# Batch 1's second product by Strassen's algorithm, with the loads, transposes and read-outs around it put in another order

## The chip, the cores and the metric

One core of one Trainium2 chip runs the kernel. The time is device microseconds of one execution; the figure compared is the median over runs. Beside each set of runs one execution is profiled, and the views below are of that one.

The engines are named as in the profile: PE is TensorE (PEld its weight loads), DVE is VectorE, ACT is ScalarE, POOL is GpSimd, SP is SyncE. SP and POOL issue DMAs in their own instruction order.

## The reference

Cross attention between tokens and a small state, and then a feed-forward layer with exact Gelu, over all rows that the attention gives.

```python
B, H, S, Ns, D = 8, 8, 512, 32, 64
scores  = x @ state^T / 8            # per batch and head, S x Ns
xread   = softmax(scores)  @ state   # S x D
scores2 = state @ x^T / 8            # Ns x S
sread   = softmax(scores2) @ x       # Ns x D
rows    = concat([xread, sread], rows).reshape(8 * 544, 512)
out     = gelu(rows @ w_in) @ w_out  # w_in 512 x 2048, w_out 2048 x 512
```

## The kernel before, in words

All matrix operands are bf16, sums are fp32 in PSUM. The kernel never forms xread. For each batch b it forms P = state x w_in, head by head (256 rows for pairs of heads and states, 2048 columns, `Ps[b]`), and multiplies the softmax weights by it: hidden = A x P.

The steps of one batch are these.

- `load_x` (L115, a DMA that POOL issues and that casts to bf16), `rearr` (L214, POOL, into `x4`), `xtr_dma` (L269, a transpose by DMA that SP issues, into `xT`), and `rearr_ones` (L223, POOL for batch 2 and later, into `xo`, the operand of the read-out). There are two `xb` buffers, so batch b + 2 is loaded when `rearr` and `rearr_ones` of batch b are done.
- `load_st` and `state_prep` (L149): state, transposed by PE and put into `sbd` by DVE.
- `scores` (L316): x times state on PE; ACT takes exp into `e`. Exp and Gelu need different tables of ACT, so two table loads surround it.
- `norm` (L338): sum, reciprocal and product on DVE, giving the weights `a`; `atr` (L354, PE and DVE, batches 0 and 1) or `atr_dma` (L364, a transpose by DMA that SP issues) turns them into A^T.
- P in four chunks f of 512 columns: `p_mm` (L409) issues eight small matmuls in a 64x32 tiling of PE into two PSUM banks, `p_copy` (L424) copies one on ACT and one on DVE. Several chunks in a row are a P run (`burst`, L435, and `p_run`, L796).
- `M(m)` (`mm1`, L473): the first product, sixteen column blocks m of 128 per batch, each two matmuls of 512 columns on PE and one Gelu on ACT, into `gs[b]`.
- the second product, gs[b] x w_out. Batches 0 and 1 do it plainly: `U(u)` (`mm2`, L499) is four matmuls of 512 columns for a quarter q of the sum and a row block j; `mm2_m` (L527) does the same numbers by column block m. Units 0 to 15 are batch 0, 16 to 31 are batch 1. Each row block is copied by DVE (L491) and written out by SP. Batches 2 to 7 do it by Strassen's algorithm: `X(b, name)` (L611), seven products named 1 to 7, of sixteen matmuls of 256 columns each. `g_sum` (L577, DVE) makes the sums of quarters of gs[b] that five of them need, and `w_sums` (L554, DVE) the five sums of quarters of w_out, once.
- `sread` (L372): the read-out of the state rows, 32 small matmuls in a 128x32 tiling; `sread_out` (L386, DVE) divides by the sums, and `srt` (L399, PE and DVE) transposes into `XSR`, which is multiplied by w_in and w_out for all batches together in the course of batch 7.

PSUM has eight banks. Four rotate (`ftile`, tag f: M, scores, read-outs, transposes, some P chunks), so an instruction that takes a bank waits until the one four back has been read. Four have names (`otile`, o0 to o3: the second product and the other P chunks).

The order on every engine is written out by hand in the body: engines run their instructions in that order and wait where an operand or a buffer isn't ready. The start loads w_in and w_out in chunks on POOL's queue; from batch 2 on a loop over b and eight steps p does `M(k, k + 1)` in each step and hangs the rest on it: for the next batch, nb = b + 1, scores in p = 1, norm in p = 2 and 3, P runs in p = 5 and 7, and for the last batch its products X in p = 0 to 4. `hold` is a one-element POOL copy that reads a Gelu output, so that the loads behind it start no earlier.

Of the kernel before, what the change touches and what calls it, by code (L numbers as in the profile page):

```python
# [17 lines left out]
def kernel(  # L18
# [8 lines left out]
    nc = tc.nc  # L27

    B, H, S, D = x.shape
# [73 lines left out]
    def load_w_in(f0, f1):  # L103
        for t in range(2):
            nc.gpsimd.dma_start(  # L105
                out=w_in_bf[64 * t:64 * t + 64, :, f0:f1],
                in_=moe_w_in[256 * t:256 * t + 256, f0:f1].rearrange("(c d) f -> d c f", c=HC),
            )
# [3 lines left out]
    def load_w_out(i):  # L112
        nc.gpsimd.dma_start(out=w_out_bf[:, 4 * i:4 * i + 4, :], in_=w_out_r[:, 4 * i:4 * i + 4, :])
# [6 lines left out]
    def load_st(b0, b1):  # L120
        nc.gpsimd.dma_start(
            out=st_bf[:, b0:b1, :, :].rearrange("q b t d -> q (b t) d"),
            in_=st_rows[:, b0:b1, :, :].rearrange("q b t d -> q (b t) d"),
        )
# [7 lines left out]

    def load_rest():
        load_w_out(1)
        for f in range(2, FC):
            load_w_in(512 * f, 512 * f + 512)
            load_w_out(f)
        load_st(2, B)
        load_x(2)
        load_x(3)  # L140


# [289 lines left out]

    def burst(chunks, b_read=None):  # L435
        done = []
        first = len(chunks) < 4 and b_read is not None
        if first:
            sread(b_read)
        for i, (b, f) in enumerate(chunks):  # L440
            done.append((b, f, p_mm(b, f, ftile if i < 2 else otile)))
        for x in done[:2]:
            p_copy(*x)
        if b_read is not None and not first:
            sread(b_read)
        for x in done[2:3]:
            p_copy(*x)
        if b_read is not None:
            sread_out(b_read)
        for x in done[3:]:  # L450
            p_copy(*x)


    def pmat00(h):
        if h == 0:
            Ps[0] = att.tile([128, 2, d_ff], BF16, name="P", tag="P")
# [42 lines left out]
    def mm2(b, q, j):  # L499
        if q == 0:  # L500
            ops[b, j] = otile([128, d_model], "op")
        ps = ops[b, j]
        for m in range(4 * q, 4 * q + 4):
            nc.tensor.matmul(  # L504
                ps,
                lhsT=gs[b][:, m, j * 128:(j + 1) * 128],
                rhs=w_out_bf[:, m, :],
                start=(m == 0),
                stop=(m == MC - 1),
            )  # L510
        if q == 3:
            rows = out_rows(b, j)
            evac(ps, [(rows, slice(0, 128), 0, d_model)])

    def mm1_sr(m):
        hp = ps_f.tile([128, B * NS], FP32, name="hps", tag="f")
# [276 lines left out]
            nc.vector.tensor_tensor(out=rs["o", 0][:, :NH], in0=ps, in1=rs["u"], op=add)  # L793
            r_out(0)

    def p_run(b, fs, banks):  # L796
        done = []
        for f, at in zip(fs, banks):
            it = iter(at or ())
            tiles = (lambda shape, name: otile(shape, name, next(it))) if at else ftile  # L800
            done.append((b, f, p_mm(b, f, tiles)))
        for x in done:
            p_copy(*x)


    def M(*ms):
# [77 lines left out]
    srt(0)  # L884
    U(4, 5)
    rearr_ones(1)
    U(6)
    pmat(0, 2)
    norm(1, 0)
# [4 lines left out]
    sread_out(1)  # L894
    M(10, 11)
    mm2_m(0, 8)
    mm2_m(0, 9)
    burst([(0, 3), (1, 0)])
    mm2_m(0, 10)
    atr(1)  # L900
    M(12, 13)
    srt(1)
    M(14, 15)
    mm2_m(0, 11)
    begin(2)
    rearr(2)
    xtr_dma(2)
    rearr_ones(2)
    U(12)
    burst([(1, 1), (1, 2)])  # L910
    U(13)
    state_prep(2, B)
    M(16, 17)
    U(14)
    M(18, 19)
    U(15)
    burst([(1, 3), (2, 0), (2, 1)])
    U(16)


    M(20, 21)
    U(17)
    nc.gpsimd.tensor_copy(out=hold, in_=gs[1][:, 4, 0:1])
    load_x(4)
    w_sums(0)
    pmat(2, 2)
    begin(3)
    rearr(3)
    xtr_dma(3)
    rearr_ones(3)  # L930
    M(22, 23)
    scores(2, 0)
    scores(2, 1)
    U(18)
    norm(2, 0)
    norm(2, 1)
    M(24, 25)
    U(19)
    M(26, 27)
    U(20, 21)  # L940
    w_sums(1)
    M(28, 29)
    w_sums(2)
    U(22)
    atr_dma(2)
    M(30, 31)
    U(23)
    pmat(2, 3)
    w_sums(3)
    w_sums(4)  # L950

    u = 24
    for b in range(2, B):
        nb = b + 1
        for p in range(8):
            k = 16 * b + 2 * p
            if p == 1 and nb < B:
                scores(nb, 0)
                scores(nb, 1)
            if p in (2, 3) and nb < B:  # L960
                norm(nb, p - 2)
            if p == 3 and nb + 1 < B:
                xtr_dma(nb + 1)
            if p == 5 and nb < B:
                atr_dma(nb)
            if p == 6 and nb < B:
                srt(b)
            if p == 7 and nb == B - 1:
                srt(nb)
            M(k, k + 1)  # L970
            if b == 2:
                for _ in range(2 if p < 4 else 1):
                    if u < 32:
                        U(u)
                        u += 1
            elif p < 5:
                if p == 0:
                    g_sum(b - 1, "5")
                X(b - 1, "45127"[p])
                if p < 3:  # L980
                    g_sum(b - 1, "127"[p])
            if nb == B and p < 4:
                for m in range(4 * p, 4 * p + 4):
                    mm1_sr(m)
            if p == 1 and nb < B:
                sread(b)
                sread_out(b)
            if p == 4 and nb == B - 1:
                sread(nb)
                sread_out(nb)  # L990
            if p == 0 and b + 3 < B:
                nc.gpsimd.tensor_copy(out=hold, in_=gs[b][:, 0, 0:1])  # L992
                load_x(b + 3)
            if p == 0 and nb + 1 < B:
                begin(nb + 1)
                rearr(nb + 1)
            if p == 2 and nb + 1 < B:
                rearr_ones(nb + 1)
            if nb == B:
                if p == 4:  # L1000
                    r_homes()
                    r_sum("5")
                    r_sum("2")
                if p == 5:
                    g_sum(b, "6")
                    R("3")
                    r_sum("1")
                    R("4")
                    r_sum("6")
                    r_sum("7")  # L1010
                if p == 6:
                    R("5")
                    X(b, "3")
                    R("2")
                    R("1")
                if p == 7:
                    R("6")
                    X(b, "6")
                continue
            if p == 5:  # L1020
                g_sum(b, "6")
                if nb < B:
                    p_run(nb, (0, 1), ((0, 1), (3, 2)))
            if p == 6:
                X(b, "3")
            if p == 7:
                if nb < B:
                    p_run(nb, (2, 3), ((1, 2), None))
                X(b, "6")
    b = B - 1  # L1030
    for name in "521":
# [39 lines left out]
```

## Time and profile before

| | us |
|---|---|
| median of 8 runs | 206.97 |
| lowest and highest | 206.28, 207.75 |
| the profiled execution | 207.45 |
| its span, first to last instruction | 205.7 |
| PE busy | 198.6 |
| DVE busy | 138.2 |
| ACT busy | 132.8 |
| POOL busy | 62.2 |

The profiled execution has 1.75 us around its span. The granted PE clock is 1.0 throughout. PE's busy time is modelled from overlapping matmuls: the time that a matmul really takes from PE is read from the distance between the starts of neighbours. Every time in the views counts from the start of the span.

### The profile page before, as it was taken

The numbers are of one execution on the slowest core, as the hardware profiler recorded it, in microseconds if no ns is written. First come the engines' busy times: TensorE is split into PE (matmuls) and PEld (weight loads), VectorE is DVE, ScalarE is ACT, GpSimd is POOL, SyncE is SP. The second block draws the span as 40 slices with busy tenths as digits, with TensorE's granted clock in tenths as the row PEclk, the third lists the DMA queues.
The fourth block names the chain that finished last, engine by engine and source line by source line (L and its number), as shares of the span: only waits on it lengthen the run. The fifth ranks groups of instructions, "written<-read, shape, count | busy, mean of one in ns | idle before, by whom it ended". The sixth has DMA issues, their size and how long they took to land.

```text
span 205.7 us, 4708 instructions
## 1 busy us (share of the span) xinstructions
PE 198.6 (97%) x1971; PEld 130.8 (64%) x1979; DVE 138.2 (67%) x219; ACT 132.8 (65%) x240; POOL 62.2 (30%) x69
## 2 busy tenths in 40 slices
PE   8689999999999999999999999999999999999994
PEld 7444444444454567766775777667775788778893
DVE  2843675785739848995699858765878553165883
ACT  3874675679794879575956787587747566744120
POOL 8955300746063005720677006500220002200000
PEclk9999999999999999999999999999999999999999
DMA  6999999689664908745682502460106001030125
GB/s 198 185 174 203 206 198 194 108 235 132 128 76 124 248 13 102 158 149 59 71 173 92 129 0 78 100 183 3 53 3 204 3 0 51 3 153 0 54 94 162
DMA packets 40261, 23.14 MB, mean 113 GB/s; under 512 B 21808, under 2 KB 38320, under 8 KB 40240
## 3 DMA queue, kind: packets, MB, share of 16 engines
q0 software_dynamic: 13936, 8.10, 29.2%
q1 hardware_dynamic: 25616, 14.36, 27.7%
q10 hardware_dynamic: 688, 0.39, 0.6%
q8 instruction: 15, 0.25, 0.5%
q14 instruction: 6, 0.05, 0.1%
HBM read 17.30 MB, written 8.91 MB: 127 GB/s over the span
## 4 chain that ended last, share of the span: by engine, by line
PE 86%; DMA 7%; POOL 4%; issue 1%; DVE 0%; POOLq 0%
PE xp L586 34%; PE hp L478 25%; PE op L504 9%; DMA w_out_bf<-in_moe_w_out_dram 6%; PE p_ps L415 4%; PE hps L518 3%; PE rp L762 3%; POOL w_in_bf L105 2%; PE xp L692 2%; PE op L531 2%; DMA AT<-a 2%; PE pt L324 1%; PE sr L378 1%; POOL sbd L95 1%; POOL a L309 0%
## 5 line engine op out<-in xcount | busy, mean ns | idle before, releaser
L485 ACT ACTIVATE g<-hp 128x512 bf16<-128x512 f32 x124 | 67.2, 604 | 29.8 <-PE hp L478 24.6
L478 PE MATMUL hp<-AT,P 128*128 128x512 bf16 x248 | 63.6, 379 | 0.1
L586 PEld LDWEIGHTS <-gsum 128*128 128x128 bf16 x448 | 43.4, 98 | 11.3 <-issue 2.1
L580 DVE TENSOR_TENSOR gsum<-g 128x2048 bf16<-128x2048 bf16 x30 | 39.8, 1346 | 0.1
L478 PEld LDWEIGHTS <-P 128*128 128x128 bf16 x248 | 22.7, 98 | 18.9 <-ACT P L426 0.5
L586 PE MATMUL xp<-ws,gsum 128*128 128x256 bf16 x256 | 30.6, 273 | 0.0
L427 DVE CAST P<-p_ps 128x512 bf16<-128x512 f32 x31 | 20.0, 684 | 15.0 <-PE p_ps L415 15.0
L504 PE MATMUL op<-w_out_bf,g 128*128 128x512 bf16 x90 | 22.9, 379 | 0.4 <-DMA w_out_bf<-in_moe_w_out_dram 0.2
L586 PE MATMUL xp<-ws,g 128*128 128x256 bf16 x192 | 22.9, 273 | 0.0
L586 PE MATMUL xp<-w_out_bf,gsum 128*128 128x256 bf16 x192 | 22.8, 273 | 0.0
L426 ACT CAST P<-p_ps 128x512 bf16<-128x512 f32 x31 | 17.0, 604 | 7.9 <-PE p_ps L415 7.9
L586 PEld LDWEIGHTS <-g 128*128 128x128 bf16 x192 | 18.8, 98 | 4.3
L635 POOL TENSOR_TENSOR u<-s,oh 128x512 f32<-128x512 f32 x5 | 6.3, 1266 | 48.6 <-ACT oh L632 48.6
L504 PEld LDWEIGHTS <-g 128*128 128x128 bf16 x96 | 9.1, 98 | 11.5 <-issue 1.4
L218 POOL COPY x<-xb 128x1024 bf16<-128x1024 bf16 x12 | 12.6, 1082 | 10.9 <-DMA xb<-in_x_dram 10.9
L228 POOL COPY xo<-xb 128x1024 bf16<-128x1024 bf16 x12 | 14.5, 1242 | 1.3 <-PE sr L378 1.3
L347 DVE TENSOR_TENSOR a<-e,ics 128x512 bf16<-128x512 bf16 x14 | 13.8, 987 | 0.5
L344 DVE TENSOR_REDUCE cs<-e 128x16 f32<-128x512 bf16 x14 | 9.5, 675 | 2.8 <-ACT e L331 2.8
L629 DVE TENSOR_TENSOR s<-xp,s 128x512 f32<-128x512 f32 x5 | 3.5, 692 | 11.0 <-PE xp L586 11.0
L605 POOL TENSOR_TENSOR v<-q,oh 128x512 f32<-128x512 f32 x5 | 6.4, 1285 | 14.6 <-ACT oh L637 14.6
L415 PE MATMUL p_ps<-w_in_bf,sbd 64*32 64x512 bf16 x248 | 10.3, 382 | 0.0
L992 POOL COPY hold<-g 128x1 bf16<-128x1 bf16 x3 | 0.8, 278 | 29.7 <-ACT g L485 29.7
(111 smaller groups left out, 223.1 us busy)
## 6 DMA issues: line engine op xcount, KB each, us to landing
xb<-in_x_dram POOLq DMA_DIRECT2D x7, 512.0 KB, 7.6
out_dram<-oh SPq DMA_DIRECT2D x13, 256.0 KB, 2.4
out_dram<-osb SPq DMA_DIRECT2D x10, 256.0 KB, 3.2
out_dram<-oh SPq DMA_DIRECT2D x5, 512.0 KB, 2.7
w_out_bf<-in_moe_w_out_dram POOLq DMA_DIRECT2D x4, 512.0 KB, 12.5
w_in_bf<-in_moe_w_in_dram POOLq DMA_DIRECT2D x6, 256.0 KB, 12.4
x0f<-in_x_dram SPq DMA_DIRECT2D x3, 256.0 KB, 4.1
w_in_bf<-in_moe_w_in_dram POOLq DMA_DIRECT2D x4, 128.0 KB, 4.2
```

Source lines behind the costliest of these rows:

```text
L218: nc.gpsimd.tensor_copy(out=A.x4[:, :, :, 64 * t:64 * t + 64].rearrange("p j c d -> p c j d"), in_=src[:, t],)
L228: eng.tensor_copy(out=A.xo[:, :, :, 2 + 64 * t:66 + 64 * t].rearrange("p j c d -> p c j d"), in_=src[:, t],)
L344: nc.vector.reduce_sum(out=cs, in_=e4, axis=AX.X)
L347: nc.vector.tensor_tensor(out=A.a[:, :, hs].rearrange("p g (c n) -> p g c n", n=NS), in0=e4, in1=ics[:, :, :].to_broadcast((128, G, 2, NS) ...
L415: nc.tensor.matmul(ps[t][32 * c:32 * c + 32, :], lhsT=sbd[64 * t:64 * t + 64, b, c, 32 * t:32 * t + 32], rhs=w_in_bf[64 * t:64 * t + 64, c ...
L426: nc.scalar.copy(out=dst[:, 0, :], in_=ps[0])
L427: nc.vector.tensor_copy(out=dst[:, 1, :], in_=ps[1])
L478: nc.tensor.matmul(hp, lhsT=Ps[b][:, t, m * 128:(m + 1) * 128], rhs=atts[b].AT[:, :, t, :], start=(t == 0), stop=(t == 1),)
L485: nc.scalar.activation(out=gs[b][:, m, :], in_=hp, func=AF.Gelu)
L504: nc.tensor.matmul(ps, lhsT=gs[b][:, m, j * 128:(j + 1) * 128], rhs=w_out_bf[:, m, :], start=(m == 0), stop=(m == MC - 1),)
L580: nc.vector.tensor_tensor(out=t, in0=g_q(b, h0, k0), in1=g_q(b, h1, k1), op=op)
L586: nc.tensor.matmul(ps[:, j - js[0], :], lhsT=lhs[:, m, 128 * j:128 * j + 128], rhs=rhs[:, m, :], start=(first and j == js[0] and m == 0), ...
```

## The change

Batch 1's second product leaves the plain form (units 16 to 31) and takes the seven products X(1, ...), two of them ahead of the loop and five in the loop's first pass. The order of loads, P chunks, sums of w_out and transposes ahead of the loop is rewritten: state of batch 2 and x of batch 2 are loaded ahead of the last chunk of w_out, x of batch 3 behind it, the states of batches 3 to 7 later; the transpose of x of batch 3 stands ahead of that of A of batch 2. x of batches 4 and 5 is loaded in the loop's first pass, in p = 0 and p = 6. In the loop the read-out moves from p = 1 (and, for batch 7, p = 4) to p = 5, directly ahead of the P run there, with its division behind the run's copies; its transpose moves from p = 6 to p = 7, and `rearr_ones` from p = 2 to p = 5. Batch 0's last row block is copied and written in two halves.

```diff
--- before.py
+++ after.py
@@ -132,11 +132,12 @@
 
     def load_rest():
         load_w_out(1)
-        for f in range(2, FC):
-            load_w_in(512 * f, 512 * f + 512)
-            load_w_out(f)
-        load_st(2, B)
+        load_w_in(1024, 1536)
+        load_w_out(2)
+        load_w_in(1536, 2048)
+        load_st(2, 3)
         load_x(2)
+        load_w_out(3)
         load_x(3)
 
 
@@ -432,25 +433,6 @@
 
 
 
-    def burst(chunks, b_read=None):
-        done = []
-        first = len(chunks) < 4 and b_read is not None
-        if first:
-            sread(b_read)
-        for i, (b, f) in enumerate(chunks):
-            done.append((b, f, p_mm(b, f, ftile if i < 2 else otile)))
-        for x in done[:2]:
-            p_copy(*x)
-        if b_read is not None and not first:
-            sread(b_read)
-        for x in done[2:3]:
-            p_copy(*x)
-        if b_read is not None:
-            sread_out(b_read)
-        for x in done[3:]:
-            p_copy(*x)
-
-
     def pmat00(h):
         if h == 0:
             Ps[0] = att.tile([128, 2, d_ff], BF16, name="P", tag="P")
@@ -510,7 +492,8 @@
             )
         if q == 3:
             rows = out_rows(b, j)
-            evac(ps, [(rows, slice(0, 128), 0, d_model)])
+            h = d_model // 2 if j == SJ - 1 else d_model
+            evac(ps, [(rows[:, n:n + h], slice(0, 128), n, n + h) for n in range(0, d_model, h)])
 
     def mm1_sr(m):
         hp = ps_f.tile([128, B * NS], FP32, name="hps", tag="f")
@@ -793,14 +776,21 @@
             nc.vector.tensor_tensor(out=rs["o", 0][:, :NH], in0=ps, in1=rs["u"], op=add)
             r_out(0)
 
-    def p_run(b, fs, banks):
+    def p_run(b, fs, banks, copy=None):
         done = []
         for f, at in zip(fs, banks):
             it = iter(at or ())
             tiles = (lambda shape, name: otile(shape, name, next(it))) if at else ftile
             done.append((b, f, p_mm(b, f, tiles)))
         for x in done:
-            p_copy(*x)
+            (copy or p_copy)(*x)
+
+    def p_copy_v(b, f, ps):
+        for t in range(2):
+            nc.vector.tensor_copy(out=Ps[b][:, t, f * 512:(f + 1) * 512], in_=ps[t])
+
+    def hold_for(b, m):
+        nc.gpsimd.tensor_copy(out=hold, in_=gs[b][:, m, 0:1])
 
 
     def M(*ms):
@@ -884,6 +874,7 @@
     srt(0)
     U(4, 5)
     rearr_ones(1)
+    w_sums(2)
     U(6)
     pmat(0, 2)
     norm(1, 0)
@@ -894,62 +885,55 @@
     sread_out(1)
     M(10, 11)
     mm2_m(0, 8)
+    p_run(1, (0, 1), (None, None))
     mm2_m(0, 9)
-    burst([(0, 3), (1, 0)])
+    atr(1)
+    pmat(0, 3)
     mm2_m(0, 10)
-    atr(1)
+    M(16, 17)
+    srt(1)
     M(12, 13)
-    srt(1)
-    M(14, 15)
     mm2_m(0, 11)
     begin(2)
     rearr(2)
     xtr_dma(2)
-    rearr_ones(2)
+    w_sums(0)
+    M(14, 15)
+    state_prep(2, 3)
+    pmat(1, 2)
     U(12)
-    burst([(1, 1), (1, 2)])
-    U(13)
-    state_prep(2, B)
-    M(16, 17)
-    U(14)
-    M(18, 19)
-    U(15)
-    burst([(1, 3), (2, 0), (2, 1)])
-    U(16)
-
-
-    M(20, 21)
-    U(17)
-    nc.gpsimd.tensor_copy(out=hold, in_=gs[1][:, 4, 0:1])
-    load_x(4)
-    w_sums(0)
-    pmat(2, 2)
     begin(3)
     rearr(3)
     xtr_dma(3)
-    rearr_ones(3)
-    M(22, 23)
+    w_sums(1)
+    M(18, 19)
+    U(13)
+    w_sums(3)
+    M(20, 21)
+    hold_for(1, 5)
+    load_st(3, B)
     scores(2, 0)
     scores(2, 1)
-    U(18)
+    U(14)
+    p_run(1, (3,), ((3, 0),), p_copy_v)
+    M(22, 23)
     norm(2, 0)
     norm(2, 1)
+    atr_dma(2)
     M(24, 25)
-    U(19)
+    p_run(2, (0,), ((1, 3),))
+    U(15)
+    X(1, "3")
+    g_sum(1, "6")
     M(26, 27)
-    U(20, 21)
-    w_sums(1)
     M(28, 29)
-    w_sums(2)
-    U(22)
-    atr_dma(2)
+    hold_for(1, 12)
+    rearr_ones(2)
+    p_run(2, (1,), ((1, 2),))
+    state_prep(3, B)
     M(30, 31)
-    U(23)
-    pmat(2, 3)
-    w_sums(3)
-    w_sums(4)
-
-    u = 24
+    X(1, "6")
+
     for b in range(2, B):
         nb = b + 1
         for p in range(8):
@@ -963,17 +947,16 @@
                 xtr_dma(nb + 1)
             if p == 5 and nb < B:
                 atr_dma(nb)
-            if p == 6 and nb < B:
+            if p == 7 and nb < B:
                 srt(b)
-            if p == 7 and nb == B - 1:
-                srt(nb)
+                if nb == B - 1:
+                    srt(nb)
             M(k, k + 1)
-            if b == 2:
-                for _ in range(2 if p < 4 else 1):
-                    if u < 32:
-                        U(u)
-                        u += 1
-            elif p < 5:
+            if b == 2 and p in (0, 3):
+                pmat(2, 2 + p // 3)
+            if b == 2 and p == 1:
+                w_sums(4)
+            if p < 5:
                 if p == 0:
                     g_sum(b - 1, "5")
                 X(b - 1, "45127"[p])
@@ -982,20 +965,17 @@
             if nb == B and p < 4:
                 for m in range(4 * p, 4 * p + 4):
                     mm1_sr(m)
-            if p == 1 and nb < B:
-                sread(b)
-                sread_out(b)
-            if p == 4 and nb == B - 1:
-                sread(nb)
-                sread_out(nb)
             if p == 0 and b + 3 < B:
-                nc.gpsimd.tensor_copy(out=hold, in_=gs[b][:, 0, 0:1])
-                load_x(b + 3)
+                hold_for(b, 0)
+                load_x(4 if b == 2 else b + 3)
+            if p == 2 and b == 2:
+                rearr_ones(3)
+            if p == 6 and b == 2:
+                hold_for(b, 12)
+                load_x(5)
             if p == 0 and nb + 1 < B:
                 begin(nb + 1)
                 rearr(nb + 1)
-            if p == 2 and nb + 1 < B:
-                rearr_ones(nb + 1)
             if nb == B:
                 if p == 4:
                     r_homes()
@@ -1019,13 +999,18 @@
                 continue
             if p == 5:
                 g_sum(b, "6")
-                if nb < B:
-                    p_run(nb, (0, 1), ((0, 1), (3, 2)))
+                reads = (b, nb) if nb == B - 1 else (b,)
+                for r in reads:
+                    sread(r)
+                p_run(nb, (0, 1), ((0, 1), (3, 2)))
+                for r in reads:
+                    sread_out(r)
+                if nb + 1 < B:
+                    rearr_ones(nb + 1)
             if p == 6:
                 X(b, "3")
             if p == 7:
-                if nb < B:
-                    p_run(nb, (2, 3), ((1, 2), None))
+                p_run(nb, (2, 3), ((1, 2), None))
                 X(b, "6")
     b = B - 1
     for name in "521":
```

## The prediction

> **What bounds the kernel now.** I read the page's head first, then the chain that ended last, then the timelines of the engines around the edit.
>
> ```profile
> span 205.7 us, 4708 instructions
> PE 198.6 (97%) x1971; PEld 130.8 (64%) x1979; DVE 138.2 (67%) x219; ACT 132.8 (65%) x240; POOL 62.2 (30%) x69
> ```
>
> ```profile
> PE 86%; DMA 7%; POOL 4%; issue 1%; DVE 0%; POOLq 0%
> ```
>
> TensorE (PE) is the bound: it is 97% busy and carries 86% of the chain; DMA and POOL stand in the chain only before 22.2 us, when the second w_out chunk lands. Nothing ahead of that changes. From there PE issues almost back to back, so every microsecond of PE work or PE wait counts in full and work elsewhere counts only where it makes PE wait. The PE timeline gives the prices, read from start to start because the ends are modelled:
>
> ```profile
> 26.11 1.03 PE L478 MATMUL hp<-AT,P 128*128 128x512 bf16 x4
> 27.07 0.43 PE L378 MATMUL sr<-xo,e 128*32 128x65 bf16 x32
> 27.43 1.08 PE L478 MATMUL hp<-AT,P 128*128 128x512 bf16 x4
> 28.34 1.89 PE L531 MATMUL op<-w_out_bf,g 128*128 128x512 bf16 x7
> 30.16 0.63 PE L415 MATMUL p_ps<-w_in_bf,sbd 64*32 64x512 bf16 x16
> 30.72 1.04 PE L531 MATMUL op<-w_out_bf,g 128*128 128x512 bf16 x4
> ...
> 69.08 1.03 PE L478 MATMUL hp<-AT,P 128*128 128x512 bf16 x4
> 69.94 1.91 PE L586 MATMUL xp<-ws,g 128*128 128x256 bf16 x16
> 71.69 1.03 PE L478 MATMUL hp<-AT,P 128*128 128x512 bf16 x4
> ```
>
> Four 512-column matmuls take 69.94 - 69.08 = 0.86 us, 0.216 each; sixteen of 256 columns take 71.69 - 69.94 = 1.75 us. The read-out (sr) stands between matmuls that should end at 26.11 + 0.86 = 26.97 and the next at 27.43: 0.46 us for 32 small matmuls. A P run of two chunks costs 30.72 - 30.06 = 0.65 us (the eight matmuls from 28.34 end at 30.06; the row counts 7, a record is missing); runs of one (24.89) and three (40.95) worked out likewise cost 0.43 and 0.87. So a chunk costs 0.22 us and each entry into a run another 0.22.
>
> **What the Trainium skill says.** "TensorEngine Tiling (Array Packing)", Tiling Modes, Key Properties: "Mode switching requires drain". The trace agrees: about 0.09 us pass before the first sr (26.97 to 27.07) and p_ps (30.06 to 30.16) matmul, and as much again after the last; these are the 0.22. "SBUF — State Buffer", its glossary, says that VectorE (DVE) and GpSimd (POOL) take turns at a shared port pair and the loser blocks. The trace agrees in kind: one gsum of DVE takes 1.21 us at 90.13 and 1.83 us at 111.76, where POOL copies from 110.03. "DMA: Bandwidth & Descriptors", Queues, rings and completion order, says that a DMA engine alternates between the queues that have work. Here the transpose of x lands in 4.4 us at best and in 6.6 at worst, and the worst one (47.58) runs beside an x load (44.66, landed after the longest late wait, 7.6 us).
>
> **The change, part by part, on PE.**
>
> (1) Second product of batch 1. Removed: 16 units of four 512-column matmuls, 16 x 0.864 = 13.82 us. Added: seven products of sixteen 256-column matmuls, 7 x 1.747 = 12.23. Net -1.6 us.
>
> (2) P chunks of batches 0, 1 and 2 are the same number, but in nine runs instead of six after 24.8 us: three more entries, +0.65 us.
>
> (3) The read-outs of batches 2 to 6 move next to a P run. One of the two pairs of drains is shared only in part: sr and p_ps are different tilings (128x32 and 64x32), so I take one drain saved of the two that could be, 0.12 us (between 0 and 0.22), five times: -0.6. Batch 7's read-out joins batch 6's and loses its whole entry and exit: -0.22.
>
> (4) In p = 5 the P run now has 0.36 us of read-out ahead of it. Before, its second chunk waited for a bank that DVE was emptying: L415 begins at 89.89 and the next row at 90.59, 0.13 longer than the undisturbed 0.56; at 111.48 0.18 longer. Both go: -0.3.
>
> Together -2.05 us if PE never waits for anything new.
>
> **New waits.** Ahead of each I name who is late.
>
> (5) The P run of (1, 0) and (1, 1) now follows one mm2_m of 0.86 us, at 29.20, instead of two. With four banks in rotation its second tile takes the bank of the read-out sr(1), which DVE frees at 29.78:
>
> ```profile
> 28.68 0.69 DVE L347 TENSOR_TENSOR a<-e,ics 128x512 bf16<-128x512 bf16 x1
> 29.29 0.16 DVE L391 RECIPROCAL inv<-sr 128x2 f32<-128x2 f32 x1
> 29.49 0.29 DVE L392 TENSOR_TENSOR srm<-sr,inv 128x128 bf16<-128x128 f32 x1
> ```
>
> DVE is busy without a break from 25.40, so this can't come earlier; the added w_sums(2) of 1.2 us fits into DVE's idle 23.8 to 25.4. PE waits from 29.31 to 29.84: +0.53.
>
> (6) pmat(1, 2) comes one transpose after M(14, 15), and its second bank is M14's. From M14 to the bank's release are 0.22 + 0.42 (from last issue to ACT's start) + 0.60 (Gelu) + 0.05 = 1.29 us; PE arrives 1.02 us after M14. +0.27.
>
> (7) scores(2) needs x of batch 2 transposed. Moved ahead of w_out 3 in the load queue, x lands one 2.6 us transfer and most of a 1.3 us one earlier: 32.3 instead of 36.0. POOL's rearr (2.0) ends at 34.5; the transpose runs beside x of batch 3 and, priced by the 47.58 one, lands at 41.1. PE, after (5) and (6), asks at 40.8: +0.3, between 0 (a 4.4 us transpose) and 0.6. w_out 3 lands at 34.9 instead of 32.1: its first user, w_sums(0), comes up on DVE at 35.0 and its first PE user at 37.3, so it costs nothing. SP's queue holds the output of U(12) and the next transpose behind this one; four osb buffers cover that.
>
> (8) In batch 6, p = 7, two srT copies (0.72 each on DVE) hold the two banks that the last P chunk wants: DVE ends them 1.7 us after the transposes, PE is there after 1.3. +0.45.
>
> (9) In p = 5 POOL's rearr_ones now starts beside DVE's gsum, P copies and the read-out's division. srt in p = 7 wants srm 4.4 us after p = 5 begins; DVE has it after 4.0, or 4.4 if the port slows gsum. +0.15 in all, between 0 and 0.6.
>
> ACT: two table loads per batch as before; M22 to M25 wait for nothing as the exp of scores(2) frees its banks at 43.5 and 44.0, when PE asks at 43.7 and 44.1. DVE's added gsums (five of 1.2) and three adds less four evacuations of 0.69 fall in its idle third; norm(2) ends near 47.7 on DVE, its transpose (3.1 to 5.1 us) by 52.8 at the worst, and M(32) asks at 52.7: nothing. Both copies of P chunk (1, 3) go to DVE, which is free at 43.2, while ACT loads tables and reads exp. The states of batches 3 to 7 are now asked for at 42 behind hold_for(1, 5) on POOL and wanted by state_prep at 50; even the longest late landing, 7.6 us, is in time. xtr_dma(3) stands on SP near 41 and is wanted at 56. The last evacuation in two halves is one more SP issue, which nothing waits for.
>
> Waits of before that go (the A^T wait near 55 and small ones): -0.3. Sum: -2.05 + 0.53 + 0.27 + 0.3 + 0.45 + 0.15 - 0.3 = -0.65, call it **-0.6 us**. The profiled execution took 207.45, 0.5 above the median of the runs, so I forecast about 206.85 for a profiled one and **206.4 us** for the median. A run of 0.3% (0.62 us) more or less is about what a measurement of this kernel can tell from no change.
>
> **Rivals.**
>
> A. The covers hold: PE doesn't wait in (5), (7), (8) and (9), for instance because the bank is another or the transposes land fast, and the sum is -2.05 - 0.3 + 0.27 and some slack for a wait of 0.7 that I don't see: 205.6 us. For it: PE is the only full engine. Against it: the DVE rows above. 25%.
>
> B. Slower. In batch 2 the load of x of batch 4 now starts just ahead of its own rearr, where before it had 13 us between them:
>
> ```profile
> 44.66 0.87 POOL L117 DMA_DIRECT2D xb<-in_x_dram  x1
> ...
> 57.27 0.87 POOL L117 DMA_DIRECT2D xb<-in_x_dram  x1
> 58.14 2.04 POOL L218 COPY x<-xb 128x1024 bf16<-128x1024 bf16 x2
> ```
>
> POOL, in order, then stands until the load lands (issued at 54.45; 5.8 to 7.6 us), and behind it are rearr (2.0), u (1.27), rearr_ones(3) (2.0) and v (1.29). DVE's add of v waits for POOL, the add of X7 behind it frees the bank that the P run of p = 5 wants at 68.5. With a landing in 5.8 us, v ends at 66.9 and the bank is free at 68.2: no wait. From 6.1 us on, each further 0.1 us of landing is 0.1 us of PE. At 7.6 us, as beside a transpose, PE loses 1.5, and DVE's backlog meets srt: -0.6 + 1.6 gives 208.0 us. Against it: the landings without a transpose beside them were 5.8 to 6.6, and no transpose runs then. 20%.
>
> C. The second product gains but nothing arrives: the waits come to the saving and the time is 207.0. 5%.
>
> **How the numbers follow.** The forecast's case has 50%, between -1.3 and +0.3 us; 30 of these are faster by over 0.62, 20 within. Case A is faster, C within, B slower in all but the smallest landings; I move 2 points from within to slower for waits not found. Faster 0.55, same 0.23, slower 0.22. The range reaches from A with its unseen slack (205.2) to B short of its worst (207.9); the forecast's own is 205.7 to 207.3.
>
> **What would show it.** L504 with two thirds of its rows gone and 112 more under L586; the P run near 29.3 split by 0.5 us with DVE's L392 as releaser; sr directly ahead of p_ps with a gap of 0.1; POOL's wait for xb near 54 to 60 and PE dense around 68. If PE stands over 1 us at 68, B is right; if it is dense through 29 to 42, A is. Wrong at the root is the prediction if the p = 5 pair costs more than 0.65 + 0.46 us, or if PE waits anywhere outside the places named.

## The result, and the profile after

The changed kernel takes 209.67 us (median of 11 runs, 208.57 to 210.32) against 207.0 before: 1.0122 times, 95% interval 1.0102 to 1.0142. It is slower by 1.2%; the forecast was 206.4 with a range up to 207.9. The profiled execution took 208.57, the fastest of its runs, with a span of 206.8.

The head of the page after, and its line on PE's instruction fetches (packets, MB, share of 16 engines; before it had 15 packets):

```profile
span 206.8 us, 4827 instructions
PE 198.2 (96%) x2022; PEld 136.1 (66%) x2027; DVE 142.4 (69%) x227; ACT 134.2 (65%) x242; POOL 68.7 (33%) x74
...
q8 instruction: 16, 0.26, 0.5%
```

PE's busy time fell by 0.4 us and the span grew by 1.1, so the time lies in waits and beside PE. Three places of the timeline of PE show it.

```profile
21.29 2.75 PE L486 MATMUL op<-w_out_bf,g 128*128 128x512 bf16 x11
...
67.20 0.41 PE L416 MATMUL p_ps<-w_in_bf,sbd 64*32 64x512 bf16 x8
68.41 0.37 PE L416 MATMUL p_ps<-w_in_bf,sbd 64*32 64x512 bf16 x1 [0.80 <-DVE oh L591]
69.01 0.41 PE L416 MATMUL p_ps<-w_in_bf,sbd 64*32 64x512 bf16 x7 [0.23 <-DVE oh L626]
69.35 1.04 PE L460 MATMUL hp<-AT,P 128*128 128x512 bf16 x4
70.22 1.91 PE L569 MATMUL xp<-ws,g 128*128 128x256 bf16 x16
72.33 0.23 PE L403 MATMUL srT<-ident,srm 128*128 128x128 bf16 x1 [0.20 <-DVE srm L393]
...
199.15 3.70 PE L675 MATMUL xp<-ws,gsum 128*128 128x256 bf16 x48
```

The same places before:

```profile
22.21 2.75 PE L504 MATMUL op<-w_out_bf,g 128*128 128x512 bf16 x11 [0.17 <-DMA w_out_bf<-in_moe_w_out_dram]
...
68.45 0.62 PE L415 MATMUL p_ps<-w_in_bf,sbd 64*32 64x512 bf16 x16
...
199.05 3.70 PE L692 MATMUL xp<-ws,gsum 128*128 128x256 bf16 x48
```

From unit 4 (21.29) to the start of the last 48 matmuls (199.15), called PE's path below, are 177.86 us; before, the same stretch ran from 22.21 to 199.05, 176.84. So PE's path is 1.0 us longer where the prediction had it 0.65 shorter. From that last start to the end of the span, called the tail below, are 7.65 us after and 6.63 before: another 1.0 us, behind the last product, where the prediction had nothing. The two make 2.0 of the 2.67. In this execution the second w_out chunk landed early and PE began unit 4 0.9 us sooner than in the profile of before, and so its span hides that much; a later sample of the changed kernel (a1) is 2.25 us over before. What is left, 0.2 to 0.7 us, no single place shows.

### The profile page after: what moved, and what is told of

Its sections match the earlier page's. It is cut to its first block, busy times and chain, and to the rows that moved or that the text cites. A ratio compares the mean times of both kernels' runs of the same rounds, so it can differ in the third digit from the quotient of the medians.

```text
span 206.8 us, 4827 instructions
## 1 busy us (share of the span) xinstructions
PE 198.2 (96%) x2022; PEld 136.1 (66%) x2027; DVE 142.4 (69%) x227; ACT 134.2 (65%) x242; POOL 68.7 (33%) x74
## 4 chain that ended last, share of the span: by engine, by line
PE 82%; POOL 5%; DVE 5%; issue 3%; DMA 2%; ACT 1%; SPq 0%; POOLq 0%; DVEq 0%; ACTq 0%
PE xp L569 35%; PE hp L460 23%; PE p_ps L416 4%; PE hps L501 3%; PE op L514 3%; PE op L486 3%; PE rp L745 3%; DMA x0f<-in_x_dram 2%; PE xp L675 2%; PE pt L325 1%; POOL xo L229 1%; POOL x L219 1%; POOL u L618 1%; PE sr L379 1%; DVE P L428 1%
## 5 line engine op out<-in xcount | busy, mean ns | idle before, releaser
L569 PEld LDWEIGHTS <-gsum 128*128 128x128 bf16 x528 | 51.2, 98 | 13.1 <-issue 1.9
L563 DVE TENSOR_TENSOR gsum<-g 128x2048 bf16<-128x2048 bf16 x35 | 45.5, 1316 | 0.1
L569 PE MATMUL xp<-ws,gsum 128*128 128x256 bf16 x304 | 36.3, 273 | 0.0
L569 PE MATMUL xp<-ws,g 128*128 128x256 bf16 x224 | 26.8, 273 | 0.0
L569 PE MATMUL xp<-w_out_bf,gsum 128*128 128x256 bf16 x224 | 26.6, 273 | 0.0
L569 PEld LDWEIGHTS <-g 128*128 128x128 bf16 x224 | 21.8, 98 | 5.1 <-issue 0.2
L591 DVE TENSOR_TENSOR oh<-xp,v 128x512 f32<-128x512 f32 x6 | 4.1, 691 | 11.8 <-POOL v L588 11.8
L348 DVE TENSOR_TENSOR a<-e,ics 128x512 bf16<-128x512 bf16 x14 | 10.8, 768 | 0.6 <-DVE ics L347 0.2
L624 DVE TENSOR_TENSOR q<-xp,s 128x512 f32<-128x512 f32 x6 | 4.1, 684 | 7.8 <-PE xp L569 7.8
L406 DVE COPY XSR<-srT 128x128 bf16<-128x128 bf16 x8 | 5.7, 759 | 5.2 <-PE srT L403 5.2
```

What stands on the lines that cost most here:

```text
L348: nc.vector.tensor_tensor(out=A.a[:, :, hs].rearrange("p g (c n) -> p g c n", n=NS), in0=e4, in1=ics[:, :, :].to_broadcast((128, G, 2, NS) ...
L563: nc.vector.tensor_tensor(out=t, in0=g_q(b, h0, k0), in1=g_q(b, h1, k1), op=op)
L569: nc.tensor.matmul(ps[:, j - js[0], :], lhsT=lhs[:, m, 128 * j:128 * j + 128], rhs=rhs[:, m, :], start=(first and j == js[0] and m == 0), ...
```

## The experiments

Two theories came out of the profile. PORT: in batch 2 POOL has a string of copies and sums behind the landing of x of batch 4, DVE has Strassen's sums, the two slow each other, and PE waits near 68. FETCH: PE's longer instruction stream needs one more fetch, which falls among the last output writes. The rivals: the transfer of x alone is late (LANDING); the last writes are slow because of the writes ahead of them (WRITES); the moved read-outs are what costs. Behind each time below stand its ratio to the kernel before, measured beside it, and the 95% interval of that ratio.

**a1, the changed kernel again.**

> The changed kernel itself, for a second profile: the profiled execution of it (208.57) was its fastest, 1.1 us under its median of 209.67, while the one of before was 0.5 over its median, so the two profiles explain 1.1 of the 2.7 us only. Theory POOL: the landing of x of batch 4 stands on the path (POOL waits for it, then rearr, u, rearr_ones(3) and v in a row, then DVE's two adds, then the P run of p = 5 in batch 2), so its spread goes into the time: a slower execution shows a landing over 5.8 us and a PE wait over 1.6 us at the P run near 68. Theory DMA: the rest lies in the loads ahead of 22 us or in the last output writes; then the PE wait near 68 is again about 1.6 us and the time lies before or behind it. About 209.7 in either case.

209.31 us, 1.0106 (1.0076 to 1.0137). In this profile unit 4 began at 21.76, so half of the early start of the first profile is gone, and that 0.5 us is all by which this execution (209.09) is slower than the first (208.57); PE's path is 177.72 us and the tail 7.7. x of batch 4 took 5.7 us to land and the wait near 68 was 1.5 us, both 0.1 less than in the first profile. So a later landing isn't what made this execution slower. That the two fell together fits a landing that stands on the path, but two profiles don't show it.

**a2, the load of x of batch 4 earlier.**

> Load of x of batch 4 issued straight behind rearr_ones(2), some 2.4 us earlier; nothing else is changed. Theory POOL: x lands near 57, v ends near 65.3, the bank wait of 1.6 us at the P run and the srt wait of 0.3 us behind it go: 1.6 to 1.9 us less than the changed kernel, about 207.8, and more if typical executions wait longer than the profiled one. Theory DMA: POOL's lateness is covered elsewhere and PE finds another wait in batch 2: less than 0.5 us gained, about 209.3.

```diff
     rearr_ones(2)
+    load_x(4)
     p_run(2, (1,), ((1, 2),))
...
-                load_x(4 if b == 2 else b + 3)
+                if b > 2:
+                    load_x(b + 3)
```

209.99 us, 1.0133 (1.0080 to 1.0187): nothing gained; PE's path in its profile is 177.86 us, as in the changed kernel's. The wait at the P run is gone from the PE timeline and others stand in its place:

```profile
64.09 1.03 PE L460 MATMUL hp<-AT,P 128*128 128x512 bf16 x4
65.20 1.92 PE L569 MATMUL xp<-ws,gsum 128*128 128x256 bf16 x16
66.96 0.59 PE L460 MATMUL hp<-AT,P 128*128 128x512 bf16 x2
68.48 0.59 PE L460 MATMUL hp<-AT,P 128*128 128x512 bf16 x2 [0.93 <-DVE P L428]
...
73.17 0.23 PE L403 MATMUL srT<-ident,srm 128*128 128x128 bf16 x1 [0.38 <-DVE srm L393]
```

The product (xp) begins 0.2 us late for a gsum, M(43) 1.1 us late for a bank that DVE empties, srt 0.5 us late. The reason is in the timelines of POOL and of DVE of this run:

```profile
58.05 3.34 POOL L219 COPY x<-xb 128x1024 bf16<-128x1024 bf16 x2 [4.21 <-DMA xb<-in_x_dram]
61.35 1.27 POOL L618 TENSOR_TENSOR u<-s,oh 128x512 f32<-128x512 f32 x1
62.58 3.47 POOL L229 COPY xo<-xb 128x1024 bf16<-128x1024 bf16 x2
66.01 1.27 POOL L588 TENSOR_TENSOR v<-q,oh 128x512 f32<-128x512 f32 x1
```

```profile
58.43 2.06 DVE L563 TENSOR_TENSOR gsum<-g 128x2048 bf16<-128x2048 bf16 x1
...
61.40 1.76 DVE L348 TENSOR_TENSOR a<-e,ics 128x512 bf16<-128x512 bf16 x1
...
66.06 1.76 DVE L348 TENSOR_TENSOR a<-e,ics 128x512 bf16<-128x512 bf16 x1
```

Undisturbed, a pair of copies takes 2.03 us, a gsum 1.22 and the product of norm 0.69. Here the copies of 3.34 and 3.47 us overlap gsums of 2.06 and (from 63.69) 1.46, and the two products of norm take 1.76 beside POOL's u and v. LANDING is refuted: x came earlier and the two engines spent the gain on each other.

**b1, POOL's and DVE's work taken out of that stretch.**

> The changed kernel with POOL and DVE relieved in batch 2: rearr_ones(2) and rearr_ones(3) moved ahead of scores(2), into POOL's idle 42 to 48; load of x of batch 4 at hold_for(1, 12), some 4 us earlier; w_sums(4) ahead of the loop, into DVE's idle 50 to 53. An earlier load alone (a2) gained nothing: POOL's copies then ran beside DVE's sums and each slowed the other. Theory PORT (the 1.9 us of PE waits near 68 come from POOL and DVE having together more to do in batch 2 than PE leaves time for): 2.0 us of POOL copies and 1.2 of DVE sums less in that stretch, the waits at the P run and at srt go, 1.5 to 1.9 us less than the changed kernel, about 207.8. Theory LANDING (only the transfer is late): already refuted if a2 is right; then this gains less than 0.5.

```diff
     load_st(3, B)
+    rearr_ones(2)
+    rearr_ones(3)
     scores(2, 0)
...
     hold_for(1, 12)
-    rearr_ones(2)
+    load_x(4)
     p_run(2, (1,), ((1, 2),))
     state_prep(3, B)
+    w_sums(4)
```

In return the same calls are gone from the loop's first pass. 208.55 us, 1.0066 (1.0044 to 1.0087): 0.8 to 1.1 us gained, about half of what PORT expected. PE doesn't wait near 68 any more, but it does at 49.5, 1.6 us for the evacuation of unit 15, and the timelines of POOL and DVE say why:

```profile
43.73 3.99 POOL L229 COPY xo<-xb 128x1024 bf16<-128x1024 bf16 x4
```

```profile
45.51 2.76 DVE L348 TENSOR_TENSOR a<-e,ics 128x512 bf16<-128x512 bf16 x1
```

```profile
49.52 0.39 PE L416 MATMUL p_ps<-w_in_bf,sbd 64*32 64x512 bf16 x1
51.14 0.41 PE L416 MATMUL p_ps<-w_in_bf,sbd 64*32 64x512 bf16 x7 [1.23 <-DVE osb L473]
```

POOL ran its four copies in a row from 43.73 to 47.72, and one DVE product of 0.69 us took 2.76, until just after they ended. Here it is DVE that loses: its product waits the copies out. So the wait moved with the copies. PE's path in this profile (an execution of 209.55, 1.0 over the median) is 177.49 us, only 0.4 less than the changed kernel's, so the rest of the gain in the median is in no profile.

**c1, the copies spread to where DVE reads PSUM or idles.**

> The changed kernel with POOL's work of batch 2 put where DVE reads PSUM or idles: rearr_ones(2) behind rearr(2) (near 34), rearr_ones(3) and rearr(4) at hold_for(1, 12) (49 to 53), load of x of batch 4 behind load_st(3, B) near 42, of x of batch 5 in p = 0; w_sums(4) ahead of the loop. In b1 four POOL copies in a row from 43.7 to 47.7 held one DVE product for 2.76 us instead of 0.69, and a wait of 1.6 us at the P run of 49.5 took the place of those near 68. Theory PORT: with the copies away from DVE's SBUF work neither wait is there; 1.9 us less than the changed kernel, about 207.6. If the waits near 68 had to do with batch 2's amount of work whatever the port, a wait of over 1 us stays and it is about 208.8.

```diff
     xtr_dma(2)
+    rearr_ones(2)
     w_sums(0)
...
     load_st(3, B)
+    load_x(4)
...
     hold_for(1, 12)
-    rearr_ones(2)
+    rearr_ones(3)
+    begin(4)
+    rearr(4)
     p_run(2, (1,), ((1, 2),))
     state_prep(3, B)
+    w_sums(4)
```

208.47 us, 1.0075 (1.0046 to 1.0104). Neither of the two waits is in its profile. One of 1.3 us is new: M(32) at 52.71 waits for A transposed, which SP issues at 46.30 while the load of x of batch 4 (landed 51.8) is running. Beside that load the transpose of A took 6.4 us to land instead of 3.1. So of the 1.9 us expected, 1.3 went to another wait. As in b1, POOL's copies have left the stretch altogether: the run shows that POOL's string was the cause near 68, and how much of that string is work and how much is the slowing is read from its rows (below).

**c3 and d1, all three together.** c3 is c1 with the division first (c2 below) and 48 rows fewer in PE's instruction stream (b2 below); d1 is c3 with c1's load put behind the transpose of A.

> All three together: relief as in c1, the division first as in c2, 48 fewer rows as in b2. PORT 1.9, bank 0.5, FETCH 1.0 us, less what an earlier PE loses to the transpose of x of batch 2 (0 to 1.5, as seen in one profile of b2): between 206.1 and 207.0. This is what the change can bring at its best, with Strassen for batch 1 kept; the read-out move alone (a4) stands at 206.4.

c3: 207.16 us, 1.0018 (0.9998 to 1.0038), just over its range, with 0.5 us at M(32) and 0.8 at scores(2).

> c3 with the load of x of batch 4 moved behind hold_for(1, 12) (near 49, after the transpose of A of batch 2 has landed), rearr(4) back in p = 0 of batch 2, load of x of batch 5 in p = 0 of batch 3 as x of batch 6 was... in short: rearr_ones(2) near 34, rearr_ones(3) near 49, division first, 48 warm-up rows fewer. If the causes are PORT, bank and FETCH alone, the 0.5 us wait at M(32) goes and nothing new comes: 0.5 us less than c3, about 206.5, with the wait of 0.8 at scores(2) still there. If batch 2's DVE and POOL work still collide, a wait near 65 to 70 is back and it is 207.5 or more.

```diff
# against c3
     load_st(3, B)
-    load_x(4)
...
     hold_for(1, 12)
+    load_x(4)
     rearr_ones(3)
-    begin(4)
-    rearr(4)
```

x of batch 5 is loaded in p = 0 of batch 2 here, as in c1 and c3, and not in batch 3. d1: 207.0 us, 0.9996 (0.9972 to 1.0020), not to be told from c3 and 0.5 us over its expectation; its profiled execution took 206.23. The wait at M(32) is gone, none is near 65 to 70, the one at scores(2) stays:

```profile
38.76 1.03 PE L460 MATMUL hp<-AT,P 128*128 128x512 bf16 x4
40.47 0.64 PE L325 MATMUL pt<-sbd,xT 128*128 128x64 bf16 x16 [0.68 <-ACT g L467]
```

The 0.8 us are for the transpose of x of batch 2, issued at 33.8 and landed 6.6 us later; the releaser named, a Gelu, had long been done.

**b2 and b3, the rows of PE's instruction stream.**

> The changed kernel with 24 fewer warm-up matmuls at the start (31 to 15, 12 to 4), so 48 fewer rows in PE's instruction stream; the computation is the same. In all profiles with batch 1 by Strassen a 16th instruction fetch (16 KB, 0.93 us on a DMA engine) runs while the last output is written, the last four writes land in 2.5 to 3.9 us instead of 1.65 to 2.4, and 4.2 us instead of 3.15 lie between PE's last matmul and the end. Theory FETCH: PE's stream has grown from 3960 to 4056 rows and now needs a 16th fetch; with 4008 rows it comes later or not at all, and the end is 1.0 us earlier, about 208.5. Theory WRITES: the last writes are slower for another reason (more and larger output DMAs before them): the tail stays at 4.2 us, about 209.5. Colder PE at the start may cost up to 0.5 in both.

> The kernel before with 48 small matmuls (16 columns, of zeros, results unused) in PE's waits ahead of 11 us, so that PE's stream has as many rows as the changed kernel's; the rest is the same. Theory FETCH: a 16th instruction fetch falls into the last writes, and 3.15 us from PE's last matmul to the end become 4.2: 1.0 us slower than before, about 208.0. Theory WRITES: the tail stays at 3.15 us and the time at 207.0.

```diff
# b2, the changed kernel
-    keep_warm(31)
+    keep_warm(15)
...
-    keep_warm(12)
+    keep_warm(4)
# b3, the kernel before; 16 + 8 + 24 of them
+    nc.tensor.matmul(ps[:, 0:16], lhsT=warm, rhs=warm[:, 0:16], start=True, stop=True)
```

b2: 208.66 us, 1.0078 (1.0057 to 1.0100), 0.65 to 1.0 less than the changed kernel. With fewer warm-up matmuls PE's first score matmuls of 64 columns took up to 0.26 us instead of 0.20, but unit 4 began at 21.78, as in a1. b3: 208.2 us, 1.0053 (1.0034 to 1.0071), 1.2 more than before although nothing but 48 idle matmuls was added. The DMA view of the last microseconds, first of b3, then of b2:

```profile
q8 instruction: 1, 0.02, 1.0%
issues: line engine op xcount, KB each, median us to landing
out_dram<-oh SPq DMA_DIRECT2D x1, 256.0 KB, 3.9
out_dram<-oh SPq DMA_DIRECT2D x1, 128.0 KB, 3.1
out_dram<-oh SPq DMA_DIRECT2D x1, 64.0 KB, 3.1
out_dram<-oh ACTq DMA_DIRECT2D x1, 64.0 KB, 2.6
```

```profile
q14 instruction: 1, 0.01, 0.7%
issues: line engine op xcount, KB each, median us to landing
...
out_dram<-oh SPq DMA_DIRECT2D x1, 256.0 KB, 2.6
out_dram<-oh SPq DMA_DIRECT2D x1, 128.0 KB, 1.9
out_dram<-oh SPq DMA_DIRECT2D x1, 64.0 KB, 1.7
out_dram<-oh ACTq DMA_DIRECT2D x1, 64.0 KB, 1.7
```

With a fetch of queue q8 in that window the four last writes land 0.9 to 1.4 us later. From the start of the last 48 matmuls to the end of the span are 205.9 - 198.18 = 7.7 us in b3 and 207.5 - 200.83 = 6.7 in b2, as in the changed kernel (7.65) and in that before (6.63). FETCH is shown from both sides, WRITES refuted: b3's output writes are those of before, b2's those of the changed kernel. All sixteen profiles of this document agree: the eight with a fetch behind 201 us have tails of 7.65 to 8.0 us, the eight without one 6.6 to 7.0.

**d2, the rows taken from the end of the stream.**

> d1, but with the 48 rows taken elsewhere: 32 at the end (the last two products in two pieces instead of three, 16 matmuls and weight loads fewer) and 16 at the start (31 warm-up matmuls to 23). Theory FETCH on the transpose (a fetch near 38 makes the transpose of x of batch 2 land in 6.6 us): the fetch stays near 35, the transpose lands in 5.1 and the wait at scores(2) goes, 0.8 less than d1, about 205.8; the larger last piece costs 0.1 to 0.3 at the end. If the 6.6 us have another cause, the same as d1.

```diff
# keep_warm as against the changed kernel; the second one is back at 12
-    PIECES = ((0, 0, NH, 2), (1, 0, NH // 2, 0), (1, NH // 2, NH, 1))
+    PIECES = ((0, 0, NH, 2), (1, 0, NH, 0))
...
-    keep_warm(31)
+    keep_warm(23)
```

206.27 us, 0.9980 (0.9961 to 0.9999), just under before. Its median is 0.7 less than d1's, but the two intervals overlap; in the profiles PE's path is 0.6 shorter than d1's (175.8 against 176.45) and the tail 0.3 longer. The transpose of x of batch 2 lands in 5.1 us and PE doesn't wait for it. In d1 the DMA view of 36 to 41 us has one q8 fetch; in d2 the nearest is at 35.4, ahead of most of the transpose. All three profiles with a fetch at 38 to 39 us, while the transpose runs (b2, c3, d1), show 6.6 us. b4 shows 6.2 without one, so that a fetch there is the cause is likely and not shown, and it isn't the only way to get there.

**a4 and a3, the move of the read-outs.**

> The kernel before with the move of the read-outs alone (sread, division, srt and rearr_ones as in the changed kernel). The prediction's steps (3), (4), (8) and (9) say -0.6 -0.22 -0.3 +0.45 +0.15, so 0.5 us faster than before, about 206.5; the trace of the changed kernel shows periods of 21.34 against 21.6 us in batches 3 to 5 and a bank wait of 0.12 in batch 6, so rather 0.9 faster, about 206.1. If the move costs by keeping a bank longer, it is slower than before.

```diff
# p = 1, for batch 7 p = 4
-                sread(b)
-                sread_out(b)
# p = 2
-                rearr_ones(nb + 1)
# srt(b): from p = 6 to p = 7
# p = 5
+                for r in reads:
+                    sread(r)
                 p_run(nb, (0, 1), ((0, 1), (3, 2)))
+                for r in reads:
+                    sread_out(r)
+                if nb + 1 < B:
+                    rearr_ones(nb + 1)
```

206.37 us, 0.9967 (0.9948 to 0.9985): the move alone makes the kernel before 0.7 us faster. Batch 3 in the PE timeline of a4:

```profile
87.91 1.03 PE L478 MATMUL hp<-AT,P 128*128 128x512 bf16 x4
88.87 0.43 PE L378 MATMUL sr<-xo,e 128*32 128x65 bf16 x32
89.23 0.62 PE L415 MATMUL p_ps<-w_in_bf,sbd 64*32 64x512 bf16 x16
89.79 1.04 PE L478 MATMUL hp<-AT,P 128*128 128x512 bf16 x4
```

Read-out and run together take 89.79 - 88.77 = 1.02 us, 0.09 less than 0.46 and 0.65 apart, and the run's bank wait of 0.13 is gone.

> The changed kernel with the read-outs, their division and their transposes where they were before (p = 1, for batch 7 p = 4; srt in p = 6), everything else as changed. If the move saves what the prediction says (0.12 of drain in each of five places, 0.22 for batch 7, 0.3 of bank waits, less 0.45 of bank wait in batch 6), this is 0.7 us slower than the changed kernel, about 210.4. If the move is what costs, this is faster than it by 0.5 us or more.

The diff is a4's the other way round, from the changed kernel, with rearr_ones left in p = 5.

209.48 us, 1.0115 (1.0065 to 1.0164), not to be told from the changed kernel. Its profile has the P run's waits at 68 to 70 as the changed kernel's has them, and lacks the srt wait (0.4 us) and batch 6's bank wait (0.3). These take what the move saves here: PE's path is 177.81 us without the move and 177.86 with it. The move isn't what costs.

**c2, the division of read-out 1 ahead of norm(1, 1).**

> The changed kernel with norm(1, 1) put behind the division of read-out 1 on DVE, so that the bank that the P run of (1, 0) wants is free 1.6 us earlier. Step (5) of the prediction gave this wait 0.53 us and the trace shows 0.52. If PE is the bound there, 0.5 us less, about 209.0; if the PE time gained is lost again at the next wait on a transfer (transpose of x of batch 2, near 39), nothing is gained, about 209.5.

```diff
     norm(1, 0)
-    norm(1, 1)
     U(7)
     M(8, 9)
     sread(1)
     sread_out(1)
+    norm(1, 1)
```

209.11 us, 1.0102 (1.0077 to 1.0127). The P run at 29.56 doesn't wait any more, but M(11) ahead of it waits 0.3 us for a bank that it didn't wait for before. The wait taken away was 0.3 us too: the run of the changed kernel took 0.89 us instead of 0.56 (lines below), and the 0.52 of the expectation counts in the 0.2 that a chunk takes anyway. So nothing is gained in the profile, where PE's path is 177.79 us, and the median can't be told from the changed kernel's.

**b4 and c4, batch 1 plain again.**

> The changed kernel with the second product of batch 1 plain again (units 16 to 31 at the places of the seven products: two each where X3 and X6 stand, three, three, two, two, two in p = 0 to 4 of batch 2); loads, order and read-outs stay as changed. PE has 1.6 us more work; five gsums of 1.2 us, u and v are gone. Theories PORT and FETCH together: the 1.9 us of waits near 68 and the 1.0 us of the tail (96 rows fewer) go, so 1.3 us faster than the changed kernel, about 208.2: Strassen for batch 1 costs more than it saves here. If both are wrong, it is 1.6 us slower, about 211.

> Batch 1 plain again, as b4, but with U(15) ahead of the P run of (2, 0) and that run in two rotating banks, since in b4 unit 17 waited 2.76 us for a bank that DVE was reading the P chunk from, which has nothing to do with the question. Theories PORT and FETCH: 1.6 us more PE work, 1.9 of waits near 68 and 1.0 of tail less, about 208.2. If Strassen is worth its PE time, it is over 210.

```diff
# c4; b4 leaves the first two lines as they were
-    p_run(2, (0,), ((1, 3),))
     U(15)
+    p_run(2, (0,), (None,))
-    X(1, "3")
-    g_sum(1, "6")
+    U(16, 17)
...
-    X(1, "6")
+    U(18, 19)
...
+            if b == 2 and p < 5:   # units 20 to 31: 3, 3, 2, 2, 2
+                U(...)
```

b4: 211.84 us, 1.0198 (1.0145 to 1.0252), but unit 17 waits 2.8 us for a bank of my own choosing, and behind that wait PE was slow: the eight matmuls of 512 columns from 50.35 took 2.8 us instead of 1.8, and the granted clock of that slice of the page is between 0.6 and 0.7. So it doesn't answer. c4: 209.24 us, 1.0111 (1.0080 to 1.0141). Its profile has no wait near 68; it has one of 1.0 us in the P run of (2, 0), which now uses rotating banks while ACT is busy with exp, a table load and Gelus. Less that wait it would stand at an estimated 208.2, where PORT and FETCH put it, but as run it is neither faster nor slower than the changed kernel. Whether Strassen costs more than it saves in this order is not settled by a run.

## Why the prediction was wrong

What PE was given to do came out as worked out: 112 more matmuls of 256 columns, 64 fewer of 512, batches 3 to 5 in 21.34 us each instead of 21.6 (read-out to read-out at 90.14, 111.48 and 132.82). A drain saved was 0.12 us in (3) and 0.09 in a4. Of the waits, two show in these lines:

```profile
28.38 0.95 PE L416 MATMUL p_ps<-w_in_bf,sbd 64*32 64x512 bf16 x16
29.27 1.04 PE L514 MATMUL op<-w_out_bf,g 128*128 128x512 bf16 x4
...
159.03 0.96 PE L416 MATMUL p_ps<-w_in_bf,sbd 64*32 64x512 bf16 x16
159.92 1.92 PE L569 MATMUL xp<-ws,gsum 128*128 128x256 bf16 x16
```

- (5) was 0.53. The run took 29.27 - 28.38 = 0.89 us instead of 0.56, so 0.33. Place and cause held; the size had the wait begin 0.1 us before PE was through with the first chunk.
- (6) was 0.27 and measured 0.27.
- (7) was 0.3: nothing in this profile, the transpose landed 5.1 us after its issue and PE came after it; in b2's it was 1.5 us, more than the upper bound given.
- (8) was 0.45. The run took 159.92 - 159.03 = 0.89 us, so 0.33 (a4's expectation has 0.12 for it, which is a misreading).
- (9) was 0.15 in all; from batch 3 on nothing shows, and in batch 2 the srt wait is 0.4.
- M(24) and M(25), set at nothing, wait 0.23 us together for the banks of the exp.

**The step that failed** is the working of POOL's string behind the landing of x of batch 4. It made the wait at the P run of p = 5 nothing for a landing up to 6.1 us, so that the forecast's sum has no term for it and rival B got 20%. x of batch 4 landed in 5.82 us, as taken. But POOL's work behind it was priced by rows in which DVE left the port alone:

```profile
59.27 2.48 POOL L219 COPY x<-xb 128x1024 bf16<-128x1024 bf16 x2 [4.99 <-DMA xb<-in_x_dram]
61.73 2.23 POOL L618 TENSOR_TENSOR u<-s,oh 128x512 f32<-128x512 f32 x1
63.91 2.48 POOL L229 COPY xo<-xb 128x1024 bf16<-128x1024 bf16 x2
66.35 1.28 POOL L588 TENSOR_TENSOR v<-q,oh 128x512 f32<-128x512 f32 x1
```

```profile
67.67 0.69 DVE L591 TENSOR_TENSOR oh<-xp,v 128x512 f32<-128x512 f32 x1 [2.56 <-POOL v L588]
```

From landing to the end of v, POOL took 67.63 - 59.22 = 8.4 us where the prediction added 2.0, 1.27, 2.0 and 1.29 to 6.6. The 1.8 us too many, less the 0.3 of slack that the prediction had found, are PE's wait at the P run, 1.6 us. The srt wait comes behind it, as DVE's next gsum takes 1.80 us beside rearr_ones(4). DVE was idle for 2.56 us ahead of its add of v (65.11 to 67.67), so POOL's string set the time there. The prediction had read the shared port out of the trace and "SBUF — State Buffer", applied it to DVE in (9), and left it out of the string on POOL on which rival B rests. By its own sign, PE standing over 1 us at 68, rival B came true; its cause, a landing of over 6.1 us, did not, so that it named the right place for the wrong reason.

With the measured waits in place of its own, the prediction's sum makes PE's path about 0.8 us longer: -2.05 - 0.3 + 0.33 + 0.27 + 0.33 + 0.4 + 0.23 + 1.6. Measured were 1.0.

**The second failure** is an omission: the end of the span was taken as unchanged, and its 1.0 us is the 16th instruction fetch. The page of before had shown 15 such packets of 16 KB; the change in matmuls, which the prediction counted for PE's time, was not counted for its instruction stream.

Where neither stands in the way the change does gain: d2, with both taken out, is 0.6 us faster than before, and its PE path (unit 4 at 22.84, last product at 198.66) is 175.8 us, 1.0 shorter than before. That this is the 0.6 of the forecast is in part luck, as d2 also has the division first, POOL's and DVE's work in other places and a last product in two pieces. And the read-outs' move alone gives as much (a4, 0.7 us): no run here shows that Strassen's algorithm for batch 1 gains anything on top of it.

## What to carry to other kernels

A saving on the full engine is worth what the engines feeding it can follow: before counting it, lay out the string of work on POOL and DVE in the stretch concerned and price each row as it runs beside the other, not as it runs alone. Loads moved to just ahead of their first reader put the whole string behind it on the path, and a wait taken out with a copy goes where the copy goes. Try the parts of a change one by one: here one of them, the read-outs' move, gave all that any run gained. Count the instructions too: a stream that grows past a fetch can cost a microsecond in a place that has nothing to do with the change.

## What the runs showed of the hardware

- PE's instruction fetches are packets of 16 KB on queue q8, 15 or 16 in a run of these kernels, and take 0.88 to 2.1 us each. Among the last writes one takes 0.92 to 0.96 and makes the end 1.0 to 1.2 us later; taking 48 of 4056 rows out of PE's stream (b2), or putting 96 into 3960 (b3), decides whether it comes there.
- Beside four POOL copies in a row one DVE product of two SBUF operands took 2.76 us instead of 0.69; POOL's own sum took 2.23 instead of 1.27 beside a DVE sum. PSUM reads of DVE (0.68) kept their time in the same stretch.
- A DMA transpose of x took 4.3 to 4.4 us at best, 5.1 to 6.6 beside the load of x of batch 3, and up to 6.9 (c1, beside that of batch 4); that of A took 6.4 us beside such a load (c1) instead of 3.1.
- After PE had stood for 2.6 us, matmuls of 512 columns started 0.43 us apart instead of 0.22 for about 3 us (b4, 49.1 to 52.1). After a stand of 1.2 us in b1 nothing of the kind shows. That the stand is the cause is not shown.
